# Relu² attention and an FFN on one core: the column sums of w1 move to an earlier block, and a third of the folding of g into w1 moves ahead of the first pair's second product

## The chip, the cores and the metric

One core of one Trainium2 chip runs one program. The metric is device time in microseconds. The kernel before was timed three times: 514.32, 514.0 and 515.42 us, median 514.32 us. Engines are called as in the profile: PE is TensorE (PEld its weight loads), DVE is VectorE, ACT is ScalarE, POOL is GpSimd, SP is SyncE.

## The reference

For 8 batches of 448 tokens and 12 heads of 64 (768 columns):

```python
scores = scale * (q @ k.T)
attn = np.maximum(scores, 0) ** 2 / S
x = (attn @ v), heads side by side                   # [8, 448, 768]
mu, var = mean and variance of x over the 768
xn = (x - mu) / np.sqrt(var + 1e-6) * g_ln
out = x + np.maximum(xn @ w_ch1, 0) @ w_ch2           # 768 -> 3072 -> 768
```

The kernel moves the root of the variance behind the second product (a positive factor passes through the maximum), so the first product needs only x, its mean and g.

## The kernel before

**Staging.** Batches go in pairs. Batches 0 and 1 are done in two blocks of rows each, `BLK` (L131): batch 0 in 3 and 4 of its 7 row groups of 64 (192 and 256 tokens), batch 1 in 4 and 3 (256 and 192). For each block the attention comes first (`scores`, L357: products, a ReLU on ACT, a square on DVE or ACT; `values`, L386), then the first product `xn @ w_ch1`. While PE does the first product of one block, the attention of the next block is woven in by `interleave` (L13): after each few units of the first list, a unit of the second is called. The order of the calls is the order of the instructions on every engine; nothing is reordered later.

**First product of these four blocks.** Its input is `xc` = x·g minus mean·g, in `x_room[:, b]`. `centre` (L422) makes it: six products with ones give the sum over the 768 (L430), for three of the blocks ACT copies that sum out of PSUM (L435), and six DVE instructions, one for each 128 of the 768, subtract sum·g/768 from `xc` (L437, "sweeps" below). w1 has 24 tiles of 128 columns, `ni` 0 to 23. `ffn1_head` (L696) computes tiles 0 to 2 with the loop over the six parts outermost, so that its products can start when the first sweep is done and follow the others. `ffn1` (L672) does one tile: six products into one of two PSUM buffers `ps_mm`, then a ReLU into `hT` (L692 on ACT, or L690 on DVE where the attention has just given ACT work). `ffn1_two` (L719), used in the last of the four blocks alone, does two tiles in one of three two-bank buffers `ps_sc`, with one ReLU for both (L729). `ps_sc` is also the buffer of scores, values, transposes and sums of the attention.

**Folding.** From pair 1 on, the first product takes x itself, because w1 is rewritten in place: each w1 row times its g, minus g·(column sum of g·w1)/768. Three steps lead there.

- Column sums: in the last block, `LAST = (1, (4, 3))`, the products get two more columns, the high and low part of −g/768, which lie behind the 448 tokens in `xc[1]`. After each tile DVE copies two or four numbers out of PSUM into `fold["sums"]` (L712, L713, L730, L686).
- Means: `fold_sums` (L460, three small DVE instructions), `fold_turn` (L467, one product and an ACT copy), and six `fold_mean` (L472), each with four products and one ACT copy of 512 columns.
- Folding: 36 `fold_into` (L480), one DVE instruction of 512 columns each, six for each mean. `fold_into(i, c)` rewrites part c of the tiles 2i, 2i+1, 12+2i, 13+2i.

`fold_beside` (L486) hangs turn, means and folds, and the statistics of the first tokens, on the 56 units of pair 0's second product (`ffn2`, L734), which is woven with the attention of batches 2 and 3. After each unit n its extra calls are made.

```python
units = ffn1_units(0, BLK[0][1])                                        # L1243
interleave(units[:1] + late + units[1:], attention_block(1, BLK[1][0]), 3)
fold_tiles()
interleave(ffn1_units(1, BLK[1][0]), attention_block(1, BLK[1][1]), 3, 1)
tokens(0)
```

`late` is the last four tiles of batch 0's first block. The 3 in the first `interleave` means that the last unit of the attention list, `centre`, is called when three tiles are still to come.

Of the kernel before, what the change touches and what calls it, by code (L numbers as in the profile page):

```python
# [12 lines left out]
def interleave(main, side, free=0, ahead=0):  # L13


    for unit in side[:ahead]:
        unit()
    side = side[ahead:]
    n, done = len(main) - free, 0
    for i, unit in enumerate(main):  # L20
        unit()
        want = min(len(side), (len(side) * (i + 1)) // n)
        while done < want:
            side[done]()
            done += 1
# [3 lines left out]
def kernel(  # L29
# [22 lines left out]
    nc = tc.nc  # L52
    P = 128
    HP = 64
    bf16 = mybir.dt.bfloat16
    fp32 = mybir.dt.float32

    B, H, S, D = q.shape
# [7 lines left out]
    K1 = d_model // P  # L66
    K2 = d_ff // P
# [79 lines left out]
    def load(n, names):  # L147
        if n >= len(groups):
            return
        b, m = groups[n]  # L150
        for name in names:
            if b == 1 and name != "v":
                o = (2 * m + "qk".index(name)) * 2 * S
                t = hold[:, o:o + 2 * S].rearrange("p (r s) -> p r s", r=2)
            elif name == "q":
                t = qbuf[m][:, D:D + 2 * S].rearrange("p (r s) -> p r s", r=2)
            else:
                t = slot(name, n)
            nc.gpsimd.dma_start(t, srcs[name][b][:, m:NP:G, :])  # L159
            qkv[name, b, m] = t  # L160
# [77 lines left out]
    xT, xc = {}, {}  # L238
# [90 lines left out]


    FULL = (0, J)
    FIRST, LAST = (0, BLK[0][0]), (1, BLK[1][1])
    n_early = [0]

    def busy(n):
# [6 lines left out]
    def of(blk, b=0):  # L342
        o = b % 2 * S
        return slice(o + blk[0] * HP, o + sum(blk) * HP)
# [95 lines left out]

    fold = {}

    def fold_tiles():

        t = x_room[:, 0].rearrange("p c s -> p (c s)")
        fold["means"] = [t[:, i * 1024:(i + 1) * 1024].bitcast(fp32) for i in range(2)]
        fold["sums"] = t[:, 2048:2144].bitcast(fp32).rearrange("p (n r) -> p n r", r=2)
        fold["sum"] = t[:, 2144:2192].bitcast(fp32)  # L450
        fold["rows"] = t[:, 2192:2320]
        fold["cols"] = t[:, 2320:2448]
        fold["pick"] = t[:, 2448:2448 + K2]
        nc.vector.memset(fold["rows"], 0.0)
        nc.vector.tensor_add(fold["pick"], identity[:, :K2], identity[:, K2:2 * K2])
        hi, lo = (xc[1][:, :, S + i] for i in range(2))
        nc.vector.tensor_copy(hi, g_mean)
        nc.vector.tensor_sub(lo, g_mean, hi)

    def fold_sums():  # L460

        s, rows = fold["sum"], fold["rows"]
        nc.vector.tensor_add(s, fold["sums"][:, :, 0], fold["sums"][:, :, 1])
        nc.vector.tensor_copy(rows[:, :K2], s)
        nc.vector.tensor_sub(rows[:, K2:2 * K2], s, rows[:, :K2])
# [14 lines left out]
    def fold_into(i, c):  # L480
        w = w1[:, c].rearrange("p (h n) -> p h n", h=2)[:, :, 2 * i * P:(2 * i + 2) * P]
        nc.vector.scalar_tensor_tensor(
            w, w, g_sb[:, c:c + 1], fold["means"][i % 2].rearrange("p (h n) -> p h n", h=2),
            op0=ALU.mult, op1=ALU.add)

    def fold_beside(units):  # L486

        more = {0: [fold_turn, lambda: statistics(0, 0), lambda: roots(0, 0, 1)]}
        for i, n in enumerate((1, 2, 17, 23, 30, 36)):
            more.setdefault(n, []).append(lambda i=i: fold_mean(i))  # L490
        for o in range(K2 // 4 * K1):
            more.setdefault(4 + o * 46 // 36, []).append(lambda o=o: fold_into(*divmod(o, K1)))

        def both(n, unit):
            unit()
            for f in more.get(n, ()):
                f()
        return [lambda n=n, unit=unit: both(n, unit) for n, unit in enumerate(units)]
# [147 lines left out]
    def tokens(pair):  # L646
        tokens_room(pair)
        nc.sync.dma_start_transpose(
            xt_room.rearrange("p c t d -> p (c t) d"), xT[pair].rearrange("p c s -> p (c s)"))
# [6 lines left out]
    def statistics(pair, t):  # L656
        stats = spool.tile([P, 2, nc.vector.BN_STATS_DIM], fp32, tag="stats", name="stats")
        for n in range(2):
            nc.vector.bn_stats(stats[:, n], xtok[pair][:, n * G:(n + 1) * G, t, :])  # L659
        nc.vector.bn_aggr(moments[pair][:, t, :], stats)  # L660

    def roots(pair, lo, hi):
        r = rstd[pair][:, lo:hi]
        nc.scalar.activation(r, moments[pair][:, lo:hi, 1], ACTF.Sqrt, bias=eps_sb)
        nc.vector.reciprocal(r, r)
# [6 lines left out]
    def ffn1(b, ni, blk):  # L672


        pair, o, w = b // 2, b % 2 * S + blk[0] * HP, blk[1] * HP
        if pair not in hT:
            hT[pair] = hpool.tile([P, K2, S2], bf16, tag="hT", name="hT_sb")
        ps = ps_mm.tile([P, 512], fp32, tag="mm", name="h_ps")

        more, s = 2 if (b, blk) == LAST else 0, of(blk)  # L680
        for c in range(K1):
            nc.tensor.matmul(  # L682
                ps[:, :w + more], w1[:, c, ni * P:(ni + 1) * P], xc[b][:, c, s.start:s.stop + more],
                start=(c == 0), stop=(c == K1 - 1))
        if more:
            nc.vector.tensor_copy(fold["sums"][:, ni], ps[:, w:w + more])  # L686
        since[0] += 1
        turns = 2 if (b, blk) == FIRST else 1
        if since[0] <= turns:
            nc.vector.tensor_scalar_max(hT[pair][:, ni, o:o + w], ps[:, :w], 0.0)  # L690
        else:
            nc.scalar.activation(hT[pair][:, ni, o:o + w], ps[:, :w], ACTF.Relu)  # L692
        if since[0] >= turns:
            squares_now()

    def ffn1_head(b, blk):  # L696


        pair, o, w = b // 2, b % 2 * S + blk[0] * HP, blk[1] * HP
        if pair not in hT:  # L700
            hT[pair] = hpool.tile([P, K2, S2], bf16, tag="hT", name="hT_sb")
        more = 2 if (b, blk) == LAST else 0
        s = of(blk)
        one = ps_mm.tile([P, 512], fp32, tag="mm", name="h_ps")
        two = ps_sc.tile([P, 2, 512], fp32, tag="sc", name="h2_ps")
        for c in range(K1):
            for ni, ps in enumerate((one, two[:, 0], two[:, 1])):
                nc.tensor.matmul(  # L708
                    ps[:, :w + more], w1[:, c, ni * P:(ni + 1) * P],
                    xc[b][:, c, s.start:s.stop + more], start=(c == 0), stop=(c == K1 - 1))  # L710
        if more:
            nc.vector.tensor_copy(fold["sums"][:, 0], one[:, w:w + more])  # L712
            nc.vector.tensor_copy(fold["sums"][:, 1:3], two[:, :, w:w + more])  # L713
        one, two = one[:, :w], two[:, :, :w]
        nc.scalar.activation(hT[pair][:, 0, o:o + w], one, ACTF.Relu)
        nc.scalar.activation(hT[pair][:, 1:3, o:o + w], two, ACTF.Relu)
        squares_now()

    def ffn1_two(b, ni, blk):  # L719

        pair, o, w = b // 2, b % 2 * S + blk[0] * HP, blk[1] * HP
        ps = ps_sc.tile([P, 2, 512], fp32, tag="sc", name="h2_ps")
        s = of(blk)
        for i in range(2):
            for c in range(K1):
                nc.tensor.matmul(  # L726
                    ps[:, i, :w + 2], w1[:, c, (ni + i) * P:(ni + i + 1) * P],
                    xc[b][:, c, s.start:s.stop + 2], start=(c == 0), stop=(c == K1 - 1))
        nc.scalar.activation(hT[pair][:, ni:ni + 2, o:o + w], ps[:, :, :w], ACTF.Relu)  # L729
        nc.vector.tensor_copy(fold["sums"][:, ni:ni + 2], ps[:, :, w:w + 2])  # L730

    acc = [None]

# [446 lines left out]

    def ffn1_units(b, blk):
        if (b, blk) == LAST:
            return ([lambda: ffn1_head(b, blk)]
                    + [lambda ni=ni: ffn1_two(b, ni, blk) for ni in range(3, K2 - 1, 2)]
                    + [lambda: ffn1(b, K2 - 1, blk)])
        return [lambda: ffn1_head(b, blk)] + [lambda ni=ni: ffn1(b, ni, blk) for ni in range(3, K2)]

    def late_rows(n):
# [51 lines left out]
    load(6, "qkv")  # L1240
    load(7, "qk")
    load(8, "qk")
    units = ffn1_units(0, BLK[0][1])  # L1243
    interleave(units[:1] + late + units[1:], attention_block(1, BLK[1][0]), 3)
    fold_tiles()
    interleave(ffn1_units(1, BLK[1][0]), attention_block(1, BLK[1][1]), 3, 1)
    tokens(0)
    transposed(by_dma * G + 1)
    transposed(by_dma * G + 2)
    for unit in ffn1_units(1, BLK[1][1]):  # L1250
        unit()
    fold_sums()
    side = {}

    def between_two(n):
# [145 lines left out]
```

## Time and profile before

| what | value |
|---|---|
| runs, us | 514.32 (median), 514.0, 515.42 |
| the profiled execution's own time, us | 514.53 |
| span in its trace, us | 512.7 |
| PE busy, whole span | 504.5 us, 98% |
| DVE busy | 387.3 us, 76% |
| ACT busy | 309.4 us, 60% |
| batch 0's second block (first product), about | 37.6 to 66.5 us |
| batch 1's first block | 66.5 to 87.4 us |
| batch 1's second block, the last of the four | 87.3 to 99.5 us |
| pair 0's second product with the attention of batches 2, 3 | 99.3 to 175.9 us |

The time of an execution is 1.8 us longer than the span of its trace. PE is busy nearly without a break from about 17 us on, so a time is read from the places where PE's next instruction starts later than the one before it would allow.

### The profile page before, as it was taken

The numbers are of one execution on the slowest core, as the hardware profiler recorded it, in microseconds if no ns is written. First come the engines' busy times: TensorE is split into PE (matmuls) and PEld (weight loads), VectorE is DVE, ScalarE is ACT, GpSimd is POOL, SyncE is SP. The second block draws the span as 40 slices with busy tenths as digits, with TensorE's granted clock in tenths as the row PEclk, the third lists the DMA queues.
The fourth block names the chain that finished last, engine by engine and source line by source line (L and its number), as shares of the span: only waits on it lengthen the run. The fifth ranks groups of instructions, "written<-read, shape, count | busy, mean of one in ns | idle before, by whom it ended". The sixth has DMA issues, their size and how long they took to land.

```text
span 512.7 us, 11440 instructions
## 1 busy us (share of the span) xinstructions
PE 504.5 (98%) x4553; PEld 299.0 (58%) x4553; DVE 387.3 (76%) x745; ACT 309.4 (60%) x496; POOL 129.6 (25%) x182
## 2 busy tenths in 40 slices
PE   8899999999999999999999999999999999999996
PEld 6677788855555555555555555555555555556663
DVE  5775765389899888858789968858887968868663
ACT  5966676488678266657757266639979366630000
POOL 8335112012301266321201099501100022200000
PEclk9999999999999999999999999999999999999999
DMA  9999999999969985329995989304997393322222
GB/s 196 206 207 206 211 206 159 158 145 185 190 141 166 185 197 175 130 65 168 187 245 106 186 186 184 94 11 84 188 185 173 71 215 124 94 77 63 63 61 61
DMA packets 124486, 76.31 MB, mean 149 GB/s; under 512 B 80562, under 2 KB 120498, under 8 KB 124434
## 3 DMA queue, kind: packets, MB, share of 16 engines
q1 hardware_dynamic: 93730, 41.38, 39.6%
q0 software_dynamic: 28544, 30.91, 38.3%
q10 hardware_dynamic: 2160, 3.31, 2.8%
q8 instruction: 35, 0.57, 0.5%
q14 instruction: 17, 0.14, 0.1%
HBM read 64.69 MB, written 17.89 MB: 161 GB/s over the span
## 4 chain that ended last, share of the span: by engine, by line
PE 94%; ACT 2%; DVE 1%; DMA 1%; issue 1%; SPq 0%; DVEq 0%
PE m_ps L899 28%; PE o_ps L741 20%; PE o_ps L1109 9%; PE m_ps L1109 8%; PE h_ps L682 8%; PE sc_ps L365 8%; PE av_ps L397 6%; PE h_ps L726 2%; PE h_ps L708 2%; PE o_ps L1071 2%; ACT early L376 1%; PE tr_ps L250 1%; DMA stage_sb<-in_q_dram 1%; DMA out_dram<-o_room 1%; DVE o_room L1125 0%
## 5 line engine op out<-in xcount | busy, mean ns | idle before, releaser
L376 ACT ACTIVATE attn_sb<-sc_ps 128x896 bf16<-128x896 f32 (+4 forms) x150 | 126.3, 902 | 39.4 <-PE sc_ps L365 34.5
L903 ACT ACTIVATE hT_sb<-m_ps 128x448 bf16<-128x448 f32 x144 | 78.2, 543 | 52.0 <-PE m_ps L899 49.3
L741 PE MATMUL o_ps<-w,hT_sb 128*128 128x384 bf16 x624 | 108.3, 327 | 0.0
L741 PEld LDWEIGHTS <-hT_sb 128*128 128x128 bf16 x624 | 58.2, 98 | 45.7 <-issue 10.1
L380 DVE TENSOR_TENSOR attn_sb<-attn_sb 128x896 bf16<-128x896 bf16 x98 | 61.7, 645 | 19.8 <-ACT attn_sb L376 19.1
L682 PE MATMUL h_ps<-x_room,w 128*128 128x256 bf16 (+2 forms) x384 | 43.8, 263 | 0.4 <-ACT early L376 0.3
L1109 PEld LDWEIGHTS <-hT_sb 128*128 128x128 bf16 x312 | 29.7, 98 | 22.1 <-issue 3.0
L980 DVE TENSOR_TENSOR m_ps<-x_room,m_ps 128x448 f32<-128x448 f32 x36 | 22.6, 629 | 23.8 <-ACT hT_sb L903 23.6
L682 PEld LDWEIGHTS <-w 128*128 128x128 bf16 x384 | 33.8, 97 | 7.2 <-issue 2.8
L899 PEld LDWEIGHTS <-w 128*128 128x128 bf16 x246 | 23.9, 97 | 23.1 <-issue 0.4
L1109 PEld LDWEIGHTS <-x_room 128*128 128x128 bf16 x252 | 24.2, 98 | 17.4 <-issue 1.6
L403 DVE TENSOR_SCALAR xT_sb<-av_ps 128x896 bf16<-128x896 f32 (+2 forms) x30 | 27.0, 901 | 9.3 <-PE av_ps L397 9.2
L964 ACT COPY x_room<-m_ps 128x448 f32<-128x448 f32 x36 | 19.1, 531 | 21.6 <-PE m_ps L899 20.7
L899 PEld LDWEIGHTS <-w_sum 128*128 128x128 bf16 x210 | 20.5, 98 | 19.1
L159 POOL DMA_DIRECT2D k_sb<-in_k_dram x15 | 10.7, 712 | 81.1 <-DMA kT_sb<-k_sb 57.3
L899 PE MATMUL m_ps<-x_sum,w 128*128 128x448 bf16 x120 | 29.1, 352 | 0.1
L659 DVE BATCH_NORM_STATS2 stats<-xtok_sb 128x6 f32<-128x384 bf16 x56 | 28.3, 548 | 0.0
L159 POOL DMA_DIRECT2D v_sb<-in_v_dram x20 | 14.2, 711 | 55.5 <-PE sc_ps L365 40.7
L365 PE MATMUL sc_ps<-qT_sb,kT_sb 64*64 64x448 bf16 x392 | 28.2, 358 | 0.0
L692 ACT ACTIVATE hT_sb<-h_ps 128x256 bf16<-128x256 f32 (+1 forms) x49 | 18.0, 368 | 16.1 <-PE h_ps L682 15.2
L378 ACT ACTIVATE attn_sb<-attn_sb 128x896 bf16<-128x896 bf16 x28 | 26.6, 950 | 0.9
L397 PE MATMUL av_ps<-attn_sb,v_sb 64*64 64x448 bf16 (+2 forms) x532 | 26.2, 331 | 0.1
(196 smaller groups left out, 871.7 us busy)
## 6 DMA issues: line engine op xcount, KB each, us to landing
out_dram<-o_room SPq DMA_DIRECT2D x108, 96.0 KB, 2.8
w<-in_moe_w_ch_dram POOLq DMA_DIRECT2D x12, 384.0 KB, 14.3
w<-in_moe_w_ch_dram POOLq DMA_DIRECT2D x4, 1152.0 KB, 20.0
q_sb<-in_q_dram POOLq DMA_DIRECT2D x20, 224.0 KB, 6.2
v_sb<-in_v_dram POOLq DMA_DIRECT2D x20, 224.0 KB, 6.6
k_sb<-in_k_dram POOLq DMA_DIRECT2D x15, 224.0 KB, 6.0
kept<-room SPq DMA_DIRECT2D x4, 480.0 KB, 2.6
kept<-w_sum SPq DMA_DIRECT2D x16, 96.0 KB, 1.7
```

What stands on the lines that cost most here:

```text
L365: nc.tensor.matmul(ps[cols, r, o * w:(o + 1) * w], g["k"](i)[rows, cols], g["q"](i, r)[rows, blk[0]:sum(blk), cols], start=True, stop=True)
L376: nc.scalar.activation(a, ps[:, :, :len(slots) * w], ACTF.Relu)
L378: nc.scalar.activation(a, a, ACTF.Square)
L380: nc.vector.tensor_mul(a, a, a)
L397: nc.tensor.matmul(ps[cols, hh, :w], v_sb[rows, pr, j * D:(j + 1) * D], g["attn"][i][rows, r, :], start=(j == 0), stop=(j == J - 1))
L403: nc.vector.tensor_scalar_mul(x, ps[:, :, :w], score_scale)
L659: nc.vector.bn_stats(stats[:, n], xtok[pair][:, n * G:(n + 1) * G, t, :])
L682: nc.tensor.matmul(ps[:, :w + more], w1[:, c, ni * P:(ni + 1) * P], xc[b][:, c, s.start:s.stop + more], start=(c == 0), stop=(c == K1 - 1))
L741: nc.tensor.matmul(ps[:, :DH], hT[pair][:, ki, t * P:(t + 1) * P], w2[:, ki, cols], start=(o == 0), stop=(o == K2 - 1))
L899: nc.tensor.matmul(ps, *at, start=(first and c == 0), stop=(c == KQ - 1), skip_group_check=not first)
L903: nc.scalar.activation(hT[pair][:, n + KH * row, half * S:(half + 1) * S], ps, ACTF.Relu)
L1109: nc.tensor.matmul(ps, x[:, ki], y[ki] if isinstance(y, list) else y[:, ki], start=(first and ki == 0), stop=(ki == KH - 1), skip_group_ch ...
```

## The change

`SUMS = (0, (3, 4))` becomes the block whose products carry the two more columns. They lie behind the 448 tokens of `xc[0]`; `fold_columns` writes them with two DVE instructions just ahead of that block's first product. `fold["sums"]` gets a tile of its own, since `x_room[:, 0]` is still in use. In this block the tiles are done one at a time, so 23 DVE copies replace the 13 of before, each ahead of the tile's ReLU. `fold_sums` follows that block, `fold_turn` the next one. The last block's tiles are done in another order (0 to 2, then the pairs from 12, 14, 3, 5, 16, 7, 18, 9, 20, 22, then 11); behind its first two pairs come the first two `fold_mean`, and beside the later pairs the first 12 of the 36 `fold_into`. The other four means and 24 folds stay in pair 0's second product, a fold every second unit. SP's and POOL's queues keep their instructions and order.

```diff
-    FIRST, LAST = (0, BLK[0][0]), (1, BLK[1][1])
+    FIRST, SUMS, LAST = (0, BLK[0][0]), (0, BLK[0][1]), (1, BLK[1][1])
...
-    fold = {}
+    fold = {"sums": const.tile([P, K2, 2], fp32, name="fold_sums")}
+
+    def fold_columns():
+
+        hi, lo = (x_room[:, 0, :, S + i] for i in range(2))
+        nc.vector.tensor_copy(hi, g_mean)
+        nc.vector.tensor_sub(lo, g_mean, hi)
...
-        fold["sums"] = t[:, 2048:2144].bitcast(fp32).rearrange("p (n r) -> p n r", r=2)
...
-        hi, lo = (xc[1][:, :, S + i] for i in range(2))
-        nc.vector.tensor_copy(hi, g_mean)
-        nc.vector.tensor_sub(lo, g_mean, hi)
...
-        more = {0: [fold_turn, lambda: statistics(0, 0), lambda: roots(0, 0, 1)]}
-        for i, n in enumerate((1, 2, 17, 23, 30, 36)):
+        more = {0: [lambda: statistics(0, 0), lambda: roots(0, 0, 1)]}
+        for i, n in ((2, 1), (3, 2), (4, 16), (5, 28)):
             more.setdefault(n, []).append(lambda i=i: fold_mean(i))
-        for o in range(K2 // 4 * K1):
-            more.setdefault(4 + o * 46 // 36, []).append(lambda o=o: fold_into(*divmod(o, K1)))
+        for o in range(4 * K1):
+            more.setdefault(4 + o * 2, []).append(lambda o=o: fold_into(2 + o // K1, o % K1))
...
-        more, s = 2 if (b, blk) == LAST else 0, of(blk)
+        more, s = 2 if (b, blk) == SUMS else 0, of(blk)
...
-        more = 2 if (b, blk) == LAST else 0
+        more = 2 if (b, blk) == SUMS else 0
...
-                    ps[:, i, :w + 2], w1[:, c, (ni + i) * P:(ni + i + 1) * P],
-                    xc[b][:, c, s.start:s.stop + 2], start=(c == 0), stop=(c == K1 - 1))
+                    ps[:, i, :w], w1[:, c, (ni + i) * P:(ni + i + 1) * P],
+                    xc[b][:, c, s], start=(c == 0), stop=(c == K1 - 1))
         nc.scalar.activation(hT[pair][:, ni:ni + 2, o:o + w], ps[:, :, :w], ACTF.Relu)
-        nc.vector.tensor_copy(fold["sums"][:, ni:ni + 2], ps[:, :, w:w + 2])
...
-            return ([lambda: ffn1_head(b, blk)]
-                    + [lambda ni=ni: ffn1_two(b, ni, blk) for ni in range(3, K2 - 1, 2)]
-                    + [lambda: ffn1(b, K2 - 1, blk)])
+            two, n_folds = (12, 14, 3, 5, 16, 7, 18, 9, 20, 22), 2 * K1
+
+            def unit(n):
+                ffn1_two(b, two[n], blk)
+                if n < 2:
+                    fold_mean(n)
+                for o in range(n_folds):
+                    if 1 + o * 3 // 4 == n:
+                        fold_into(*divmod(o, K1))
+            return ([lambda: ffn1_head(b, blk)] + [lambda n=n: unit(n) for n in range(len(two))]
+                    + [lambda: ffn1(b, 11, blk)])
...
+    fold_columns()
     units = ffn1_units(0, BLK[0][1])
     interleave(units[:1] + late + units[1:], attention_block(1, BLK[1][0]), 3)
     fold_tiles()
+    fold_sums()
     interleave(ffn1_units(1, BLK[1][0]), attention_block(1, BLK[1][1]), 3, 1)
+    fold_turn()
     tokens(0)
...
-    fold_sums()
     side = {}
```

## The prediction

> **What bounds the kernel.** First the page's busy times: PE works 98% of the span. Then the table of busy times for the four stages that the change touches (batch 0's second block, "SUMS"; batch 1's first; batch 1's second, "LAST"; pair 0's second product).
>
> ```profile
> PE 504.5 (98%) x4553; PEld 299.0 (58%) x4553; DVE 387.3 (76%) x745; ACT 309.4 (60%) x496; POOL 129.6 (25%) x182
> ```
>
> ```profile
> 36.00:66.50 30.50, 30.50 (x461) 23.97 (x459) 19.62 (x43) 20.13 (x41) 10.28 (x14) 1.00 1.20 208
> 66.50:87.40 20.90, 20.90 (x307) 16.99 (x304) 12.21 (x36) 14.98 (x32) 3.50 (x5) 1.00 1.24 171
> 87.40:99.50 12.10, 12.10 (x146) 12.04 (x145) 2.41 (x13) 5.97 (x13) 0.00 (x0) 1.00 1.36 181
> 99.50:176.00 76.50, 76.32 (x700) 42.03 (x698) 68.41 (x125) 54.33 (x72) 15.76 (x22) 1.00 1.14 168
> ```
>
> Columns: length, then busy us of PE, PEld, DVE, ACT, POOL, then granted clock. PE is full in all four. DVE is at 89% in the last, idle in LAST: moving folds from the one to the other looks like a gain. But a gain in the time must come out of PE, and PE has 0.2 us without work there. What can move the time is a new wait of PE. So I read the timeline where SUMS begins, in its middle and where it ends.
>
> ```profile
> 36.68 0.37 ACT L435 COPY room<-sum_ps 128x256 f32<-128x256 f32 x1 [0.33 <-PE sum_ps L430]
> 37.09 2.47 DVE L437 SCALAR_TENSOR_TENSOR x_room<-room,g_mean,x_room 128x256 bf16<-128x256 f32 x6 [0.93 <-ACT room L435]
> 37.63 2.19 PEld L708 LDWEIGHTS <-w 128*128 128x128 bf16 x18 [0.22 <-DVE x_room L437]
> 39.93 1.15 PE L682 MATMUL h_ps<-x_room,w 128*128 128x192 bf16 x12
> ```
>
> The head's 18 products start 0.06 us after the first of six sweeps (37.09 + 0.48) and follow the others.
>
> ```profile
> 43.58 1.48 PE L682 MATMUL h_ps<-x_room,w 128*128 128x256 bf16 x12
> 44.44 0.42 DVE L690 TENSOR_SCALAR hT_sb<-h_ps 128x256 bf16<-128x256 f32 x1 [1.65 <-PE h_ps L682]
> 44.78 1.36 DVE L354 TENSOR_TENSOR attn_sb<-attn_sb 128x1024 bf16<-128x1024 bf16 x2
> 45.30 0.39 ACT L692 ACTIVATE hT_sb<-h_ps 128x256 bf16<-128x256 f32 x1
> 45.90 1.49 PE L682 MATMUL h_ps<-x_room,w 128*128 128x256 bf16 x12
> 46.06 1.15 DVE L253 COPY xtok_sb<-tr_ps 128x896 bf16<-128x896 bf16 x2
> ```
>
> Tiles come in twos, 0.71 us each (12 products from 43.58 to 44.99); DVE squares and copies for the attention between them.
>
> ```profile
> 63.32 0.82 PE L430 MATMUL sum_ps<-xT_sb,ones 128*128 128x256 bf16 x6
> 63.98 2.13 PE L682 MATMUL h_ps<-x_room,w 128*128 128x256 bf16 x18
> 64.23 0.37 ACT L435 COPY room<-sum_ps 128x256 f32<-128x256 f32 x1 [0.33 <-PE sum_ps L430]
> 64.63 2.46 DVE L437 SCALAR_TENSOR_TENSOR x_room<-room,g_mean,x_room 128x256 bf16<-128x256 f32 x6 [1.31 <-ACT room L435]
> ```
>
> At the end of SUMS PE does its last three tiles (21, 22, 23) while DVE is in six sweeps. Today those tiles don't need DVE. What a copy out of PSUM does to a ReLU stands at line 686:
>
> ```profile
> L686 DVE COPY x_room<-h_ps x1: 149/149/149, 99.6 to 99.6; 128x2 f32<-128x2 f32 x1
>   ACT hT_sb L692: 0.3, 1
> ```
>
> The copy takes 0.15 us, and ACT's ReLU of the same buffer waited 0.3 us for it: they go one after the other, in the order of the code. The built program has the same wait at all of SUMS's ReLUs on ACT. [...]
>
> **1. Start of SUMS.** The two columns are written in `fold_columns` after all six sweeps, and the head's very first product reads them (x's 256 columns and two more). In the built program it waits for the second of the two writes, and the waits for single sweeps are gone. The sweeps end at 39.07 + 0.48 = 39.55. The two writes take 0.39 (the same pair at L457, L458: 67.11 to 67.50), and 0.06 follow to PE: the head starts at 40.00 instead of 37.63. It then no longer waits for sweeps: 18 × 0.1175 = 2.12, done at 42.12 instead of 39.93. **+2.2 us.** PE is in order; behind the head stand the four late tiles and the transposes, which could have filled it but come after. Bounds: 1.8 (if the columns were ready with the last sweep) to 2.4 (head no faster than its 2.30 today).
>
> **2. Middle of SUMS.** 21 copies now join DVE's queue ahead of the ReLUs. A tile's buffer must be free when the tile two later begins. I walk the queue with the durations above. (a) Tile 4 ends at 45.06, but its copy stands behind the two squares: it ends at 46.32 and the ReLU at 46.75 (45.69 before); tile 6 wants the buffer at 46.61: 0.2 late. (b) The ReLU of tile 8 is late alike, behind squares: 0.2 at tile 10. ACT's two score ReLUs (1.5 to 1.9 us together in the timeline) queue behind it, the squares behind these. (c) So tile 10's copy ends near 53.5 (in times before the start's delay) and its ReLU at 53.9; tile 12 wants it at 53.2: 0.75 late. (d) Tile 14 again behind squares: 0.2 at tile 16. (e) Today the values of the second head group start at 58.56, 0.05 after the score ReLU that frees their buffer (58.51): this ReLU is now some 2.2 late, 1.35 of it already in PE: 0.85. Sum **+2.2 us**, an estimate from these rows. Bounds: 0 (each lateness falls within the 0.5 to 1.3 us of attention products between two pairs) to 4 (0.4 at each of ten pairs).
>
> **3. End of SUMS.** `centre` is called ahead of the last three tiles, so their copies stand behind its six sweeps. Tile 23 needs tile 21's buffer. Today it starts at 65.40 (one third of 63.98 to 66.10 left). Then: sixth sweep starts 66.62, copy 67.02 to 67.18, ReLU 67.21 to 67.59, tile 23 at 67.65. **+2.25 us**; bounds 1.9 to 2.6. Queued behind it: the scores and head of the next block.
>
> **4. Gains.** The turn's product waits 0.4 us for DVE at 100.5 in the list of waits, 0.18 beyond an ordinary step: gone, since its rows are ready some 20 us earlier. In pair 0's second product two places stand out: the values at 134.11 (started 0.49 after the previous product instead of 0.18, behind a mean's ACT copy at 133.50) and scores at 164.91 (0.40 instead of 0.20). All such excess over the same stage of pair 1 sums to 0.65 us. I take **−0.4** in all; bounds 0 to −0.8.
>
> **5. At nothing.** The two columns: LAST's products take 83.5 ns for 194; two are 0.9 ns, ×144 = 0.12 us less there, the same more in SUMS. Nine products of turn and two means (0.06 each) move within PE. Twelve folds × 0.744 (row L482) = 8.9 us of DVE lie in LAST's idle 9.7: the first pair ends near 90.0, its mean's products near 90.3, a ReLU (0.49) and the mean's copy (0.58) follow on ACT, so the folds run from about 91.2 to 100.1, and the statistics behind them start where they do (100.35). Late by 2 us they would cost: their root is done at 102.14 and first used at 104.13. The two ACT copies of means (0.58) lie in ACT's 6 idle us of LAST; they share three buffers with ten tile pairs: 0 to 0.3, I take 0. The five small DVE instructions after SUMS (some 0.9 us) lie before the first square, whose score ReLU ends as late. DVE's relief in pair 0 buys nothing beyond 4. SP and POOL keep their order; their loads land where they do or wait for the later PE.
>
> **Sum:** 2.2 + 2.2 + 2.25 − 0.4 = +6.25 on the execution's own 514.53 (span 512.7 and 1.8 around it) = 520.8. That execution lies 0.2 over the median, so 520.6 beside 514.32. No later stage gives it back: PE is full to the end.
>
> **Rivals.**
> - *Only the two ordered waits.* The middle's lateness is covered by the attention's products. For it: 0.5 to 1.3 us between pairs; against: case (e) has 0.05 us of slack today. 2.2 + 2.25 − 0.4: 518.4. Chance 0.20.
> - *The middle feeds on itself.* ACT and DVE wait for each other in both directions, and each stop makes both later. Middle 5 instead of 2.2: 523.4. Chance 0.10.
> - *Faster.* DVE at 89% is what pair 0's second product suffers from, so that taking 8.9 us off it lets PE close all its gaps; decides if the first block's waits are all hidden, which needs sweeps, writes and copies to be through before PE wants them. −0.8: 513.5. Against: the head's first product cannot start before its columns are written. Chance 0.03; as much for no change.
> - *The clock falls.* The clock is 1.00 in all rows shown, and no stop of PE there is longer than 0.7 us, so no row shows what one of over 2 us does. Were the 2 us behind each of the two ordered stops at half speed, +4: 524.6. Chance 0.04. [...]
>
> **How the numbers follow.** Forecast 0.60, the others as given. The range leaves out faster, no change and the fallen clock: from the first rival less 0.8, 517.6, to the second, 523.6. A measurement of this kernel tells about 0.3% (1.5 us) from no change: faster 0.03, same 0.03, slower 0.94.
>
> **What would show it.** The head's first weight load waits for DVE at the line of the column writes, and starts 2.3 us later against its sweeps. The third of the last three tiles starts some 2.25 us late, and ACT's ReLUs in SUMS wait for DVE copies. LAST to the end keep their lengths but for 0.4 us. It is wrong if the head still follows the sweeps, if tile 23 starts on time, or if pair 0's stage is shorter by more than 1 us.

## The result, and the profile after

| | before | after |
|---|---|---|
| median of the runs, us | 514.76 (4 runs) | 522.73 (521.92, 522.01, 523.44, 523.62) |
| ratio, 95% interval | | 1.0159 (1.0143 to 1.0176) |
| the profiled execution, us | 514.53 | 521.92 |
| its span, us | 512.7 | 520.1 |

The change costs 8 us, 1.6%; 520.6 was forecast, with a range of 517.6 to 523.6. From here on, lines of the kernel after are meant where its profile is quoted (two higher than before behind `fold_columns`, for example L710 for the head's products, L684 for one tile's, L688 for the copy, L694 for the ReLU). Where an experiment adds lines, those behind them stand one to eight lines lower in the file, and its profile has the higher number. Shown timelines leave out lines of PEld and of engines that the point does not need.

The page's busy times and the table by stage, in the order of the stages that the prediction showed (columns: length, busy us of PE, PEld, DVE, ACT, POOL, granted clock, two figures on the DMAs):

```profile
PE 506.0 (97%) x4553; PEld 299.6 (58%) x4553; DVE 388.3 (75%) x755; ACT 309.0 (59%) x496; POOL 130.0 (25%) x182
```

```profile
35.40:72.80 37.40, 31.75 (x463) 24.36 (x460) 23.41 (x74) 19.95 (x42) 10.31 (x14) 0.99 1.20 208
72.80:95.00 22.20, 22.20 (x307) 17.62 (x304) 11.47 (x31) 14.90 (x31) 3.50 (x5) 0.94 0.68 101
95.00:107.20 12.20, 12.20 (x153) 12.20 (x151) 8.72 (x15) 6.73 (x16) 0.00 (x0) 1.00 1.39 161
107.20:183.20 76.00, 75.78 (x695) 41.93 (x693) 58.63 (x108) 53.28 (x69) 16.23 (x22) 1.00 1.09 172
```

Two rows are new in kind. In the first stage PE is idle for 5.65 of 37.4 us. In the second PE is full, but the stage takes 22.2 us and its granted clock is 0.94. The last two show what was wanted: DVE's folds moved (2.4 to 8.7 us in LAST, 68 to 59 in pair 0's second product), and PE's time there hardly changed.

The same products start in both traces, so the difference of their starts says where the time comes in: (us, at the first product of each place)

| place | start before | start after | difference | adds |
|---|---|---|---|---|
| first block | 22.58 | 22.18 | −0.40 | |
| SUMS, behind the head | 39.93 | 41.55 | +1.62 | **+2.0** |
| SUMS, tile 22 | 64.63 | 68.33 | +3.70 | **+2.1** |
| SUMS, tile 23 | 65.28 | 71.33 | +6.04 | **+2.3** |
| behind the next block's head | 68.47 | 76.13 | +7.66 | **+1.6** |
| LAST, from its third tile pair | 90.82 | 98.95 | +8.13 | +0.5 |
| pair 0's second product, first tiles | 100.56 | 108.36 | +7.80 | −0.3 |
| the same, near its end | 164.91 | 172.11 | +7.20 | −0.6 |

The first row lies ahead of everything that the change touches, so its −0.40 is no effect of the change; what causes it isn't shown. After the last row the difference rises to +7.35 by 192 us and stays within 0.1 of that to the end. The start of SUMS in the timeline:

```profile
36.73 2.47 DVE L437 SCALAR_TENSOR_TENSOR x_room<-room,g_mean,x_room 128x256 bf16<-128x256 f32 x6 [0.93 <-ACT room L435]
...
39.11 0.18 DVE L448 CAST x_room<-g_mean 128x6 bf16<-128x6 f32 x1
39.32 0.19 DVE L449 TENSOR_TENSOR x_room<-g_mean,x_room 128x6 bf16<-128x6 f32 x1
39.56 2.15 PE L710 MATMUL h_ps<-x_room,w 128*128 128x258 bf16 x18 [2.29 <-DVE x_room L449]
```

PE stood still for 2.29 us until the two columns were written behind the sixth sweep. The end of SUMS and what follows it:

```profile
67.66 1.48 PE L684 MATMUL h_ps<-x_room,w 128*128 128x258 bf16 x12
...
68.32 2.47 DVE L437 SCALAR_TENSOR_TENSOR x_room<-room,g_mean,x_room 128x256 bf16<-128x256 f32 x6 [0.95 <-ACT room L435]
70.70 0.22 DVE L688 COPY fold_sums<-h_ps 128x2 f32<-128x2 f32 x2
70.89 0.66 ACT L694 ACTIVATE hT_sb<-h_ps 128x256 bf16<-128x256 f32 x2 [2.60 <-DVE fold_sums L688]
71.33 0.82 PE L684 MATMUL h_ps<-x_room,w 128*128 128x258 bf16 x6 [2.18 <-ACT hT_sb L694]
...
72.81 3.49 PE L710 MATMUL h_ps<-x_room,w 128*128 128x256 bf16 x18
```

The copies of tiles 21 and 22 wait for the sweeps, the ReLUs for the copies, tile 23 for the ReLU: 2.18 us of PE. Then the next block's head takes 3.49 us for 18 products; nothing is waited for between them. Four stretches of 3.4 us around it:

```profile
65.40:68.80 3.40, 3.40 (x40) 2.88 (x33) 1.94 (x8) 1.44 (x4) 0.00 (x0) 1.00 1.16 210
68.80:72.20 3.40, 1.22 (x18) 0.77 (x19) 2.14 (x9) 0.66 (x2) 0.00 (x0) 1.00 1.26 203
72.20:75.60 3.40, 3.40 (x30) 2.27 (x27) 1.84 (x8) 1.79 (x3) 0.00 (x0) 0.50 1.26 203
75.60:79.00 3.40, 3.40 (x40) 2.74 (x39) 0.65 (x2) 2.23 (x5) 0.00 (x0) 1.00 1.28 198
```

The stretch that PE spends at 1.22 of 3.40 us busy is followed by one at half clock, 30 products instead of 40, and then by full clock again.

### The profile page after: what moved, and what is told of

It is laid out like the page before. It is cut to its first block, busy times and chain, and to the rows that moved or that the text cites. A ratio compares the mean times of both kernels' runs of the same rounds, so it can differ in the third digit from the quotient of the medians.

```text
span 520.1 us, 11437 instructions
## 1 busy us (share of the span) xinstructions
PE 506.0 (97%) x4553; PEld 299.6 (58%) x4553; DVE 388.3 (75%) x755; ACT 309.0 (59%) x496; POOL 130.0 (25%) x182
## 4 chain that ended last, share of the span: by engine, by line
PE 90%; DVE 4%; ACT 3%; DMA 1%; issue 1%; SPq 0%; DVEq 0%; ACTq 0%
PE m_ps L900 27%; PE o_ps L742 19%; PE o_ps L1110 10%; PE m_ps L1110 8%; PE sc_ps L365 7%; PE h_ps L684 6%; PE av_ps L397 6%; PE h_ps L728 2%; PE h_ps L710 2%; PE o_ps L1072 2%; ACT early L376 1%; ACT attn_sb L376 1%; DVE x_room L437 1%; PE tr_ps L250 1%; DMA stage_sb<-in_k_dram 1%; DVE xT_sb L403 1%
## 5 line engine op out<-in xcount | busy, mean ns | idle before, releaser
L376 ACT ACTIVATE attn_sb<-sc_ps 128x896 bf16<-128x896 f32 (+4 forms) x150 | 126.2, 902 | 37.4 <-PE sc_ps L365 32.3
L380 DVE TENSOR_TENSOR attn_sb<-attn_sb 128x896 bf16<-128x896 bf16 x98 | 60.0, 623 | 24.6 <-ACT attn_sb L376 23.8
L684 PE MATMUL h_ps<-x_room,w 128*128 128x192 bf16 (+2 forms) x384 | 44.7, 263 | 3.2 <-ACT hT_sb L694 2.7
L684 PEld LDWEIGHTS <-w 128*128 128x128 bf16 x384 | 33.8, 97 | 11.0 <-issue 5.9
L694 ACT ACTIVATE hT_sb<-h_ps 128x256 bf16<-128x256 f32 (+1 forms) x49 | 17.8, 368 | 20.7 <-DVE fold_sums L688 11.1
L484 DVE SCALAR_TENSOR_TENSOR w<-w,g_sb,x_room 128x512 bf16<-128x512 bf16 x36 | 25.6, 737 | 3.0 <-ACT x_room L480 3.0
```

What stands on the lines that cost most here:

```text
L376: nc.scalar.activation(a, ps[:, :, :len(slots) * w], ACTF.Relu)
L380: nc.vector.tensor_mul(a, a, a)
L684: nc.tensor.matmul(ps[:, :w + more], w1[:, c, ni * P:(ni + 1) * P], xc[b][:, c, s.start:s.stop + more], start=(c == 0), stop=(c == K1 - 1))
```

## The experiments

Four explanations are set against each other. Theory A is the sum of the terms in the table: three waits, one fall of the clock, less what the folds' move saves. Theory B says that the 23 copies load DVE, and that the time is their sum. Theory C says that the slow head comes from transposing DMAs beside it, not from the clock. Rival D says that late DMAs, not the clock, spread the executions.

Each set of runs was timed beside the kernel before, whose medians were 514.09 to 514.76 us; the ratios are to it. The granted clock behind a time is the share of full speed that PE had, as a mean over that execution: 3.413 us at half speed take 0.0033 from it in 520 us, so beside the slow end of an execution (half clock for the last 2.07 us in the trace of the kernel before, 0.81 us in that of the kernel after) 0.996 is about one such fall and 0.993 about two.

**Columns early.** `fold_columns` is called behind the first attention block.

```diff
     first_block()
+    fold_columns()
...
-    fold_columns()
     units = ffn1_units(0, BLK[0][1])
```

> Only change to the kernel after: the two columns are written right behind the first attention block, well ahead of the sweeps. Theory A (four terms: the head waits for the columns, 2.0 us; tiles late behind DVE's squares, 2.0; the last tile waits for copies behind the sweeps, 2.4; the clock halved for 3.4 us behind that stop, 1.6; folds -0.3): the head follows its sweeps again and 2.0 us go, 520.7 beside 522.7; the end's stop stays, and with it the clock's fall, or without it if the fall comes and goes with when the stop falls, 519.1. Theory B (the 23 copies simply load DVE, and the time is their sum and what they push aside): nothing changes, 522.7.

Measured: 518.44 us (517.92 to 521.53), ratio 1.0085 (1.0056 to 1.0113). The head starts with the first sweep again, and its product after it stands where the kernel before has it (difference −0.4 to −0.5 from the first block to there); the other two waits are unchanged (2.18 us at tile 23, below). B falls: no copy was moved, and some four us went.

```profile
37.10 2.47 PE L710 MATMUL h_ps<-x_room,w 128*128 128x258 bf16 x18
...
69.18 0.82 PE L684 MATMUL h_ps<-x_room,w 128*128 128x258 bf16 x6 [2.18 <-ACT hT_sb L694]
69.93 0.52 PE L365 MATMUL sc_ps<-qT_sb 64*64 64x192 bf16 x16
70.39 2.14 PE L710 MATMUL h_ps<-x_room,w 128*128 128x256 bf16 x18
```

The same stop of 2.18 us, but this time the next head takes 2.14 us: in the profiled execution (517.92) the clock did not fall. The others are 518.07, 518.08, 518.44 at a granted clock of 0.998 or more, and 519.47, 519.93, 521.53 at 0.995 to 0.997. The last is some 2 us more than one fall explains.

**The last three copies on ACT.**

```diff
-            nc.vector.tensor_copy(fold["sums"][:, ni], ps[:, w:w + more])
+            copy = nc.scalar.copy if ni >= K2 - 3 else nc.vector.tensor_copy
+            copy(fold["sums"][:, ni], ps[:, w:w + more])
```

> Only change to the kernel after: the copies of the last three tiles of the block are made by ACT, just ahead of their ReLUs, so that they don't stand behind the six sweeps. Theory A: the stop of 2.2 us at tile 23 goes, and with it the slow 3.4 us of the next block's head: 522.7 - 2.4 - 1.6 = 518.7; 520.3 if the clock falls behind the other stop, at the head, instead. Theory B: 3 of 23 copies moved, at most -0.6: 522.1. Theory C (the next head's slow products come from the transposing DMAs that start beside them, not from the clock): the head stays slow, 520.3.

Measured: 519.22 us (517.77 to 519.62), ratio 1.0077 (1.0051 to 1.0102). The stop at tile 23 is gone: its three tiles are one run of 2.18 us, and the differences of starts there go from +5.17 to +5.29 only. Taking 3 of 23 copies off DVE saved some 3.5 us, which B cannot give. Three runs lie at 517.77 to 518.01 with the full clock, four at 519.31 to 519.62 with 0.995 to 0.997, and one at 519.12 with the full clock, which A does not explain. In the profiled execution (519.31) the clock fell behind the other stop instead, at the head of SUMS:

```profile
37.30:40.70 3.40, 1.12 (x11) 1.00 (x12) 2.19 (x7) 0.33 (x1) 1.53 (x3) 1.00 1.26 204
40.70:44.10 3.40, 3.40 (x21) 2.75 (x19) 0.32 (x2) 1.31 (x3) 3.18 (x4) 0.50 1.27 203
```

**Both.** The columns are early and the last three copies are on ACT.

> Columns early and the last three copies on ACT. Theory A: only the lateness in the middle is left, 522.7 - 2.0 - 2.4 - 1.6 = 516.7, granted clock as in the kernel before (0.998). Theory B: 522.1.

Measured: 516.2 us, ten runs between 516.05 and 516.38, ratio 1.0028 (1.0007 to 1.0048). The granted clock is 0.998 to 1.0; from the head of SUMS on PE has no stop over 0.7 us, the clock does not fall before the last microseconds, and the runs hardly spread. Only the middle is left: the difference of starts goes from −0.4 behind the head to +1.65 at tile 22, 2.1 us, and to +1.34 at the end after the later saving.

**Copies beside the ReLU.** The columns are early, and every copy is made on the engine that makes the tile's ReLU, so that no ReLU waits for another engine.

```diff
+        if more:
+            copy = nc.vector.tensor_copy if since[0] <= turns else nc.scalar.copy
+            copy(fold["sums"][:, ni], ps[:, w:w + more])
```

(behind `turns`, in place of the DVE copy; the head's two copies also become `nc.scalar.copy`, and `fold_columns` is moved as above)

> Columns early, and each copy made by the engine that makes the tile's ReLU (ACT for the head and most tiles, DVE where DVE does the ReLU), so that no ReLU waits for the other engine. Theory A: all three stops and the clock's fall go, and the fold's gain is left: the kernel before less 0.3, 514.4 beside 514.8. Theory B: DVE is relieved of most copies, the same 514.4 (A and B are told apart by the other three). A third way: 16 copies of some 0.2 us on ACT make the score ReLUs late instead: 515 to 517.

Measured: 515.39 us (514.03 to 516.14), ratio 1.0008 (0.9988 to 1.0028): no difference from the kernel before that these runs tell. SUMS and the block behind it now cost 0.4 us (difference of starts −0.34 before them, +0.03 at LAST's head), against 8.1 in the kernel after. One tile of it, in the timeline:

```profile
52.84 0.16 ACT L691 COPY fold_sums<-h_ps 128x2 f32<-128x2 f32 x1 [1.02 <-PE h_ps L684]
52.89 0.39 ACT L695 ACTIVATE hT_sb<-h_ps 128x256 bf16<-128x256 f32 x1
```

On ACT the copy puts the ReLU off by 0.05 us. At the end of pair 0's second product this kernel is 0.51 us ahead of the kernel before, and 0.4 of that goes in the next stage:

```profile
176.73 0.62 DVE L754 SCALAR_TENSOR_TENSOR o_room<-o_ps,rstd_sb,xtok_sb 128x384 f32<-128x384 f32 x1 [0.57 <-DMA out_dram<-o_room]
177.26 0.61 DVE L968 TENSOR_TENSOR x_room<-x_room,m_ps 128x448 f32<-128x448 f32 x1
...
177.93 0.73 PE L901 MATMUL m_ps<-x_sum,w 128*128 128x448 bf16 x3 [0.25 <-DVE x_room L968]
```

DVE waits for a store to leave an output buffer, what is behind it on DVE is late, and PE with it. The same execution loses 0.4 more by 192 us, where PE's weight loads wait for POOL's writes of `w_sum`, and 0.6 at 293 us behind the same kind of DVE instruction; so it ends 0.9 us behind the kernel before.

**The stop filled.** In the kernel after, 36 products of ones with ones go into PE's queue ahead of tile 23. They write a free buffer, and their result isn't used.

```diff
+        if more and ni == K2 - 1:
+            fill = ps_sc.tile([P, 2, 512], fp32, tag="sc", name="fill_ps")
+            for _ in range(36):
+                nc.tensor.matmul(fill[:, 0, :P], ones, ones, start=True, stop=True)
```

> The kernel after, with 36 products of ones with ones (128 columns, some 2 us in all, into a free PSUM buffer, result unused) put into PE's queue ahead of the last tile of the block, where PE stands still for 2.2 us. The wait itself stays. Theory A (the clock is halved for 3.4 us when PE did too little in a stretch of that length): the clock no longer falls behind this stop and the next block's head takes 2.0 us again, not 3.3; 520.3 to 520.7 in executions where it does not fall at the other stop (at the head), 521.9 to 522.2 where it does; none at 523.5. Theory C (the head's products are slowed by the transposing DMAs beside them): the head stays slow, 521.9 to 523.6 as in the kernel after.

Measured: 522.1 us (521.67 to 522.45), ratio 1.0146 (1.0121 to 1.0171). No run is near 523.5, and the next block's head takes 2.14 us:

```profile
70.53 2.17 PE L686 MATMUL fill_ps<-ones 128*128 128x128 bf16 x36
...
72.39 1.34 SPq L312 DMA_TRANSPOSE kT_sb<-k_sb  x1
...
73.85 2.31 SPq L317 DMA_TRANSPOSE qT_sb<-q_sb  x1
...
74.08 2.14 PE L714 MATMUL h_ps<-x_room,w 128*128 128x256 bf16 x18
```

The transposing DMAs are still issued beside this head, as in the kernel after (there at 72.28 and 73.75), and it is fast: C falls. In the profiled execution the clock fell at the unfilled stop at the head of SUMS (half clock from 40.71 to 44.12: the head's 18 products took 2.99 us, against 2.15 in the profile of the kernel after), so the total moved little.

> As with the end filled, and 36 such products ahead of the block's head too, where PE waits 2.3 us for the columns. Theory A: the clock falls nowhere in the body, all executions within 0.5 us of each other at 520.2 to 520.7, against 521.9 to 523.6 in the kernel after. Theory C: 521.9 to 523.6.

Measured: 521.77, 522.39, 524.11 and 524.53 us, ratio 1.0177 (1.0145 to 1.0209). The clock stayed up in the profiled execution and in two others, but the times did not fall as expected; the profiled execution had a stop of 1.0 us at 375 us behind a store, and the run of 524.53 has a granted clock of 0.995, so the clock fell there in spite of the filling or at a place that no trace shows. The four runs decide nothing, so this kernel was run again with the kernel after beside it (below).

**Folds back.** This is the kernel with the copies beside the ReLU, but all means and folds are in pair 0's second product, as before. Of the change only the early sums are left.

> Columns early and copies beside the ReLUs, as in the version that took away all three stops, but with all six means and 36 folds back in pair 0's second product and the last block's tiles in their old order: of the change only the early sums are left. Theory A (the folds' move is worth 0.3 us of PE up to the end of that product): PE gets there 0.3 us later than with the folds moved, and the time is within 0.3 of the kernel before. If DVE's relief were worth more than that, 1 us or more slower than the version with the folds moved.

Measured: 514.89 us (514.12 to 516.21), ratio 1.0006 (0.9988 to 1.0024). Its starts go from −0.1 at LAST's head to −0.41 at 100.7 us, where the turn no longer waits, and stay there to 180 us. With the folds moved they went from 0.0 to −0.51 over the same stretch. So of the half microsecond that PE gains there, some 0.3 comes with the early sums and 0.2 with the folds' move. By 192 us this kernel is back at −0.06 (POOL waits 5.11 us and DVE 1.21 us for a DMA out of `w_sum`, and PE's weight loads up to 0.58 us for POOL's writes behind it); in the total nothing is left that can be told.

> The version that took away all three stops, with pair 0's 24 folds ended eight units earlier (unit 42 instead of 50). In that version PE stood still 0.4 us at the start of pair 1's first product, behind a DVE instruction that waited 0.57 us for a store from one of the three output buffers. If the late folds are behind that stop, it goes and the time falls by 0.4; if it is the store, it stays and the time is the same within 0.3.

Measured: 514.54 us (514.04 to 515.43), ratio 1.0005 (0.9992 to 1.0017). PE is 0.60 us ahead from 165 to 300 us, with no stop at 177 this time; another of 0.7 us comes at 320 us, behind statistics before which DVE stood still 1.08 us, with nothing in the profile that it waited for. At 177 us DVE does not wait for a store here, as expected if the late folds were behind that stop. But such stops come and go between executions and one execution was traced, so whether the folds or the store were behind the 0.4 is not told apart.

**Clock against time.** Three kernels were run on one chip: the kernel after, that with both stops filled, and that with columns early and the end's stop filled.

> The kernel after, unchanged, beside the next two on one chip, to have enough executions to read the granted clock against the time. Theory A: they fall into groups by the granted clock, some 521.9 (one fall of the clock, 0.996 to 0.997) and some 523.5 (two, 0.993 to 0.994), 1.6 us apart; any without a fall (0.998 and up) at 520.3. Rival D (late stores, not the clock, spread the executions): no relation of time and granted clock.

> Both stops filled, a second time, with more executions. The first time the clock stayed up, but the executions spread from 521.8 to 524.5; the profiled one had 1.2 us of another stop late in the kernel, behind a store. Theory A: the lower executions lie at 520.3 to 521.0, below the lower ones of the kernel after (521.9); the higher ones are late stores. If filling costs as much as the clock's fall, the lower ones lie at 521.9 too.

> Columns early, so no stop at the head, and the stop at the last tile filled with 36 products. With columns early alone the executions were of two kinds: 517.9 to 518.4 at a granted clock of 0.998 or more, and 519.5 to 521.5 at 0.995 to 0.997. Theory A: the second kind goes, all within 517.8 to 518.6 but for single ones with a late store. Rival D: both kinds stay.

| kernel | us, with granted clock |
|---|---|
| after | 521.68 (0.996), 521.77 (0.996), 522.71 (0.995), 523.36 (0.993), 523.63 (0.993), 526.99 (0.993) |
| both stops filled | 520.54 (1.0), 520.99 (1.0), 521.1 (0.999), 521.17 (1.0), 521.6 (0.999) |
| columns early, end filled | 517.99 to 518.16 in nine runs, 519.08 in one; 0.998 to 1.0 in all |
| columns early alone (above, another chip) | 517.92 to 518.44 in four runs (0.998 to 1.0), 519.47 to 521.53 in three (0.995 to 0.997) |

Ratios to the kernel before: 1.0164 (1.012 to 1.0208), 1.0117 (1.0084 to 1.015), 1.0051 (1.0024 to 1.0077). A's groups are there: 521.7 with about one fall, 523.5 with two; with both stops filled the five runs of this set have no fall, and all five lie below all six of the kernel after (by 0.1 us at the closest). In the third kernel the slow kind is gone. D holds for what is left: the profile of the kernel after (522.71) has a stop of 0.8 us at 186 us behind a store, and 526.99 is not explained by its clock. The waits themselves are not filled away: 520.5 to 521.6 is still some 6 us over the 514.7 of the kernel before.

## Why the prediction was right, and where it was short

1. *The start of SUMS, +2.2.* Right: the head waited for L449 and started 2.33 us late (2.37 by the working); 2.0 is left behind it. Its 18 products took 1.99 us to the next one, not 2.12. Columns early takes exactly this term away.
2. *The middle, +2.2.* Right as a sum (2.1) and place by place. At tiles 6, 10, 12, 16 and the values of the second head group the starts fell behind by 0.11, 0.18, 0.72, 0.22 and 0.60; the working had 0.2, 0.2, 0.75, 0.2, 0.85. Two it had not seen were small: 0.12 at the second late tile, 0.06 at the last values. The largest, at tile 12:

```profile
54.27 0.69 DVE L354 TENSOR_TENSOR attn_sb<-attn_sb 128x1024 bf16<-128x1024 bf16 x1 [0.23 <-ACT attn_sb L376]
54.88 0.15 DVE L688 COPY fold_sums<-h_ps 128x2 f32<-128x2 f32 x1
...
55.06 0.38 ACT L694 ACTIVATE hT_sb<-h_ps 128x256 bf16<-128x256 f32 x1 [0.83 <-DVE fold_sums L688]
55.50 0.82 PE L684 MATMUL h_ps<-x_room,w 128*128 128x258 bf16 x6 [0.56 <-ACT hT_sb L694]
```

   Square, copy, ReLU, product, each behind the one before. Copies on the ReLU's engine take all but 0.3 of this term away.
3. *The end of SUMS, +2.25.* Right: 2.34. Moving three copies takes it away. No run shows the lower bound of 1.9; in SUMS ACT's ReLUs waited for DVE's copies 12 times, 11.1 us in sum and 2.6 at the most.
4. *Gains, −0.4.* Right in size: LAST takes 0.4 more for the turn and the two means, pair 0's second product 0.9 less, and 0.2 of that is lost by 192 us, where POOL and DVE wait for a DMA out of `w_sum`: −0.3 from the head of batch 1's first block to the end. The turn's wait is gone.
5. *At nothing.* Right for LAST: PE is full there, 12.20 of 12.20 us, with the folds beside it. The folds' DVE time bought nothing beyond point 4, as the rows said: PE had no gaps to close.
6. *The clock.* This is the step that failed. The rival "the clock falls" was worked out for both stops and given 0.04, and the sum kept the full clock behind them. That was the author's estimate, and no run shows the term: no row of before has a stop of that length, and the kernel after was at a granted clock of 0.993 to 0.997 in its four runs. In the profile of the kernel after the clock fell once, behind a stop of 2.18 us, and cost 1.6 us (the rival had put each fall at 2); the runs at 523.5 have the granted clock of two falls (0.993). The sum of the other terms (2.0 + 2.1 + 2.3 − 0.3 = 6.1, that is 520.6 on the execution's 514.53) is what the kernel takes with both stops filled in the second set of runs, 520.5 to 521.6; the rest to 522.7 is mostly the clock. The first set with both filled (521.8 to 524.5, three of four at full clock) does not fit; late DMAs may be behind it, and that was not shown. PE had not stood still for the whole 3.4 us ahead of a fall: it was busy for 1.12 to 1.23 us of them, 33 to 36%, in three traces (last section).

That 522.7 lies in the range all the same is in part luck. The room above 520.6 had been left for a middle that feeds on itself, at 523.4 (the range ends at 523.6, a little above the rival that it names). The middle did not do that (2.1 us); the clock, which had been put at nothing, took the room.

## What to carry to other kernels

A small instruction added to a queue cost what stood ahead of it here, not its own 0.15 us: ask which long group of instructions it lands behind, and who waits for it (here six sweeps and a PSUM buffer, 2.3 us of PE for copies of two columns). Write constants for a chained product before the instructions that the product follows (worth 2.0 us here), and let the engine that reads a PSUM buffer anyway also make the small copy out of it (on ACT it put the ReLU off by 0.05 us). Where PE is full, taking work off another engine is worth the gaps of PE that it closes (8.9 us of DVE's folds moved here, for some 0.2 us of PE), and a new stop of PE may cost more than its length: here stops of 2.2 and 2.3 us cost up to 1.6 us more through the clock.

## What the runs showed of the hardware

Clock changes. In the trace of the kernel after, the record of the granted clock begins at 3.92 us with the full clock, which lasts 68.267 us; the half clock lasts 3.413 us, and the full clock after it 443.733 us, nearly to the end. In the trace of the kernel before, the full clock lasts 505.173 us without a break. The three full stretches are 20, 130 and 148 times 3.4133 us. The stop at tile 23 (2.18 us) and that at the head (2.29 us) are as long in every trace shown that has them unfilled. These are the stops with the 3.4 us that held most of each (in the kernel after counted in steps of 3.413 us from 3.92 us):

| trace | stop | the 3.4 us, us | PE busy | next 3.4 us |
|---|---|---|---|---|
| last three copies on ACT | head | 37.30 to 40.70 | 1.12 us, 33% | half clock (0.50) |
| end filled | head | 37.30 to 40.71 | 1.15 us, 34% | half clock (the head took 2.99 us) |
| kernel after | tile 23 | 68.77 to 72.18 | 1.23 us, 36% | half clock (0.50) |
| kernel after | head | 38.05 to 41.46 | 1.90 us, 56% | full clock (1.00) |

In the trace of columns early the stop at tile 23 (67.00 to 69.18 us) was followed by no fall: the next head took 2.14 us, and the granted clock is 0.998. So the same stop cost 1.6 us more in one execution and nothing more in another. What decides between the two is not settled by these traces.

Late DMAs. Stops of PE of 0.3 to 1.0 us come in different places of the last 350 us, in the traces above behind a store (0.25 us at 177.9 in that with the copies beside the ReLU, 0.78 at 186.2 in the kernel after, again, 1.01 at 376.5 with both stops filled) or behind statistics before which DVE stood still (0.72 at 320.3 with the folds ended earlier); runs of the kernel before reach 519 us (519.09, 519.43) at a granted clock of 0.998 or more. What makes them late stays open.
